# Slot product and inverse over n1 in the layer's two PSUM banks, with the products of the transform gathered behind the logits

## The chip, the cores and the metric

The kernel runs on one core of one Trainium2 chip. The metric is the device time of one execution in microseconds (us); lower is better. TensorE (PE) multiplies, ScalarE (ACT), VectorE (DVE) and GpSimd (POOL) work elementwise, SyncE (SP) issues the transfers. Each engine has its own list of instructions, and semaphores tie them together.

## The reference

The input is a batch of 8 sequences of 3072 tokens with 256 features. A Fourier filter runs over each sequence, then a layer with squared ReLU, then a mixture of experts with soft slots, whose softmax over all 24576 tokens decides what goes into each of 32 slots:

```python
X = np.fft.rfft(x, axis=1)
y = np.fft.irfft(X * F, n=x.shape[1], axis=1)          # filter, per sequence
h = np.maximum(x @ w_in, 0.0)                          # x: 24576 x 256
x = (h * h @ w_out)                                    # 24576 x 256
logits = x @ phi                                       # 24576 x 32
d = softmax(logits, axis=0); slot_input = d.T @ x      # slots from all tokens
...                                                    # 8 experts on 4 slots each
c = softmax(logits, axis=1); out = c @ slot_out
```

## The kernel before, in words

A sequence of 3072 = 128 x 24 tokens is transformed in two steps: over n1 (128 points) and over n2 (24 points), each a matrix product on TensorE. The way there is `mm_a` (over n1) and `mm_b` (over n2), then the filter is applied (`filt` on DVE, `join` on POOL), and the way back is `mm_g2` (over n2) and `mm_y` (over n1). Between `mm_a` and `mm_b` and between `mm_g2` and `mm_y` the data goes out to HBM and comes back in another order (`store_a`, `load_s2`, `store_g2`, `load_g`). Sequence 0 has a path of its own at the start; sequences 1 to 7 are transformed while the layer works on the sequence before.

The layer takes chunks of 512 tokens, 48 in all, and in each chunk 8 pairs P of 128-wide blocks of the hidden features. For each of the two blocks k of a pair, six full-array products (lines L594 to L596; `layer`) sum into PSUM bank `p0` or `p1`, of which there is one each. `square` then reads the bank: ReLU on ACT (L601), and the square on ACT for k = 0 (L603), on POOL for k = 1 (L605). The next pair's product for the same k waits until L601 has read the bank. DVE transposes the squares (`turn_h`, L622), and `logit` (L663) multiplies them with a folded weight; it uses 32 columns of the array at a time, four products side by side. `mm_b`, `mm_g2`, `mm_a`, `mm_y` and `slot_in` also divide the array, each in its own shape.

Per chunk c there is further work (`dispatch_events`): `evac_l`, `gather`, `emax`, `expo`, `turn_l`, `turn_e` make the weights of the softmax, `slot_in` (L794) multiplies them with the squares, which SP has moved into another layout (`move`), and `accum` (L855, DVE) adds the result to a running sum. `mm_y` (L514) gives the next chunk's input: `even_y` (L522, ACT) copies one half, `unfold` (L531, DVE) makes sum and difference, `lead_y` (L539, ACT) and `rest_y` (L546, POOL) split the result into a high and a low part.

The order is written by hand in a time of its own: a pair lasts 2 units, a chunk 16, a sequence 96. `put(t, fn, ...)` places a step at time t. `pair` calls `run_streams` before and after each of its four parts; it issues what is due, and a step with a product only where enough of the five spare PSUM banks (`side`) are free, by the table `take`. The logits of a chunk stand at times 1.5 and 9.5 (modulo 16); at 9.5 `slot_in` and `mm_y` follow them. The three products `mm_a` of a sequence, its four pairs of `mm_b` and its four `mm_g2` are placed by the numbers in `when`, and the loads that belong to them stand `LEAD` units earlier.

Of the kernel before, what the change touches and what calls it, by code (L numbers as in the profile page):

```python
# [6 lines left out]
F32 = mybir.dt.float32  # L7
# [13 lines left out]
CH = 512  # L21
NCB = N // CH
NCH = NB * NCB
# [15 lines left out]
def body(tc, x, cA, cAf, fwp, fwd, ivp, inv, flt, cst, w_in, w_out, phi, w1, w2, out):  # L39
# [10 lines left out]
    G = {}  # L50
# [32 lines left out]
    def put0(t, fn, *a):  # L83
        ev0[round(t, 3)].append((fn, a))
# [24 lines left out]
    def side():  # L109
        if G["nsd"]:  # L110
            return G["ps"].tile([128, 512], F32, tag="sd", name="sd", bufs=G["nsd"])
        k = free.pop(0)
        p = G["ps"].tile([128, 512], F32, tag=f"s{k}", name="sd")
        taken[id(p)] = k, p
        return p
# [7 lines left out]
    def fft_events(b, pl, put, TA, TB, TG, n, st):  # L123
# [263 lines left out]
        if b == 0:  # L387
# [21 lines left out]
            for i in range(8):  # L409
                put((.38, .4, .42, .44)[i] if i < 4 else F(i - 4) + 2.6, load_f, i)  # L410
                T = (16.8, 17.2, 20, 22.4, 24.9, 25.3, 27.4, 27.8)[i]
# [9 lines left out]
                T = (31.1, 33.6, 36.1, 38.6, 41.2, 44.7, 45.9, 42.4)[i]  # L421
# [5 lines left out]
        for s, (TL, TF, T) in enumerate(TA):  # L427
            put(TL, load_x, s)
            for k in range(2):
                put(TF + k, fold_x, s, k)  # L430
                for g in range(2):
                    put(T + 0.5 + (0 if T % 16 == 6 else 0.5) * k, evac_a, s, k, g)
                put(T + 2 + 0.5 * k, store_a, s, k)
            put(T, mm_a, s)
        LW, LV, LF, LS = n["lead"]
        for j in range(4):
            T = TB[j]
            for k in range(2):
                i = 2 * j + k
                put(T - LW[j], load_w, i)  # L440
                put(T, mm_b, i)
                for r in range(2):
                    put(T + 0.5 + 2 * k + r, filt, i, r)
                    put(T + 1 + 2 * k + r, join, i, r)
                put(TG[j] - LV[j], load_v, i)
            put(T - LF[j], load_f2, j)
            put(T - LS[j], load_s2, j)
            T = TG[j]
            put(T, mm_g2, j)
            for c in range(4):  # L450
                put(T + 0.5 + 0.5 * (c // 2), evac_g2, j, c)
            put(T + 3, store_g2, j)

    def out_events(b, st, late):

# [47 lines left out]

        def mm_y(g):
            t = st["gi", g]
            st["y", g] = p = [side() for e in range(2)]
            for a in range(4):
                for k in range(2):
                    for e in range(2):
                        for d in range(2):  # L510
                            rows = slice(64 * e, 64 * e + 64)
                            o = 128 * k + 64 * d
                            y = p[e][64 * d:64 * d + 64, D * k:D * k + D]
                            pe.matmul(  # L514
                                y.rearrange("p (q a t) -> p a q t", q=2, a=4)[:, a], t[rows, a, o:o + 64],
                                cI[rows, 0:64],
                                start=True, stop=True, skip_group_check=True, tile_position=(64 * e, 64 * d),
                            )
# [29 lines left out]
        for g in range(NCB):  # L548
            if 6 * b + g not in (0, 1, 6):
                T = 96 * b + 16 * g - 6.5  # L550
                late(max(T - 19.5, 13.5), load_g, g)
                late(T, mm_y, g)
                late(T + 0.5, even_y, g)
                late(T + 1, unfold, g, ALU.add)
                late(T + 1, unfold, g, ALU.subtract)
                for k in range(2):
                    late(T + 2 + 2 * k, lead_y, g, k)
                    late(T + 2.5 + 2 * k, rest_y, g, k)
                continue
            T = 96 * b + 16 * g - 4  # L560
            put = late
            if T < 0:
                def put(t, fn, *a):
                    put0(ST["G0"] + ST["Gd"] * (t + 7), fn, *a)
            put(T - (3 if T < 0 else 5), load_g, g)
            if T < 0:
                put(T - 1, warm)
            for k in range(2):
                put(T + k, mm_ai, g, k)
                put(T + k + 0.5, lead_ai, g, k)  # L570
                put(T + k + 0.5, rest_ai, g, k)
# [126 lines left out]
    def dispatch_events(c, put):  # L698
        q = 16 * (c + 1) + (2 if c else 6)
        st = {}  # L700
# [84 lines left out]

        def slot_in():

            st["S"] = S = side()
            e, h = st["eT"], hd.pop(c)
            for t in range(4):  # L790
                for n in range(4):
                    o = 4 * (n % 2)
                    v = h[:, n // 2, :, o:o + 4, 32 * t:32 * t + 32].rearrange("p r f j -> p f r j")
                    pe.matmul(  # L794
                        S[32 * n:32 * n + 32, :], e[:, 32 * t:32 * t + 32], v,
                        start=(t == 0), stop=(t == 3), tile_position=(0, 32 * n),
                    )
# [90 lines left out]
        if c == 0:  # L888
            for t, fn in zip(FIRST, (evac_l, gather, emax, expo, turn_l, turn_e, slot_blocks)):
                put(t, fn)  # L890
        else:
            put(q + .5, evac_l)
            put(q + 1.5, gather)
            put(q + 2.5, emax)
            put(q + 4, expo)
            put(q + 4, turn_l)
            put(q + 5, rescale)
            put(q + 5.5, turn_e)
        if c == 0:
            for r in range(4):  # L900
                put(FIRST[-1] + 1 + .5 * r, keep_block, r)
            put(FIRST[-1] + 3.5, sum_blocks)
        else:
            put(q + 7.5, slot_in)
            put(q + 9, accum)
        put(q + 11, row_max)
        put(q + 13, row_exp)
        put(q + 14, row_out)
# [118 lines left out]
    streams = {"dsp": [], "mv": [], "late": [], "fft": [], "w": []}  # L1027
    heads = dict.fromkeys(streams, 0)

    take = {"warm": 1, "mm_a": 4, "mm_b": 2, "mm_g": 4, "mm_g2": 4, "mm_ai": 1, "mm_y": 2, "gather": 1, "slot_in": 1, "slot_blocks": 4, "sum_blocks": 1, "turn_wo": 1, "mm_wf": 1}  # L1030

    def takes(fn, a):
        if fn is conv_wo and a[1] in (6, 7, 10):
# [3 lines left out]
    def stream(nm, o=0):  # L1037
        def put(t, fn, *a):
            streams[nm].append((t + o, fn, a))
        return put  # L1040
# [68 lines left out]
    with tc.manual_schedule():  # L1109
        put, late = stream("fft"), stream("late")  # L1110
        st = {}
        put0(43.3, load_const)
        fft_events(0, lambda: first, put0, 0, 0, 0, None, st)
        out_events(0, st, late)
        def wput(t, *a):

# [18 lines left out]
        for n in range(4):  # L1135
# [2 lines left out]
                wput(WO[n][1][k], conv_wo, n, k)  # L1138

        LEAD = [  # L1140
            [[6.5, 6.5, 9.5, 9.5], [10, 7.5, 8, 10], [5, 6, 6.5, 6.5], [5.5, 10.5, 10, 10]],
            [[5.5, 7.5, 15.25, 15.25], [6.5, 12.5, 13.5, 13.5], [5, 5.5, 10, 10], [5.5, 13, 15.25, 15.25]],
            [[20.25] + [15.25] * 3, [13.5] * 4, [20.5, 10, 10, 10], [8, 15.25, 15.25, 15.25]],
        ]

        opened = False
# [6 lines left out]
        for b in range(1, NB):  # L1153
            st = {}
            if b == 1:
                when = ([(22, 24.5, 26.5), (24, 29, 33.5), (27.5, 32, 36.5)], [47, 54.5, 65.5, 76.5], [53, 61.5, 70.5, 81.5])
            elif b == 2:
                when = ([(-19, -15.5, -10), (-11, -7, -3), (-5.5, -3, 0)], [13.5, 22, 38, 54], [18.5, 33.5, 49.5, 65.5])
            else:
                when = ([(-41, -31, -26), (-28, -22.5, -14.5), (-22.5, -15.5, -10)], [1.5, 22, 38, 54], [17.5, 33.5, 49.5, 65.5])  # L1160
            fft_events(b, lambda: G["fft"], stream("fft", 96 * (b - 1)), *when, dict(f=3, u=8, c=2, lead=LEAD[min(b, 3) - 1]), st)
            out_events(b, st, late)
        for c in range(NCH - 1):
            dispatch_events(c, stream("dsp"))
            if c:
                for n in range(4):
                    t = 0.5 * (n // 2)
                    for q, p in enumerate((12.5, 13.5, 14.5, 18) if c == 1 else (10, 11, 14, 18)):
                        stream("mv", 16 * c)(p + t, move, c, q, n)
# [10 lines left out]
        def bank(tag):  # L1180
            return G["ps"].tile([128, 512], F32, tag=tag, name="pt")
# [41 lines left out]
        for P in range(NP + 2):  # L1223
# [16 lines left out]
            if P > NP - 8:  # L1240
                j, odd = divmod(P - NP + 7, 2)
# [18 lines left out]
            evac_l, gather, emax, expo, rescale, turn_e, turn_l, slot_blocks, keep_block, sum_block,  # L1260
            row_max, row_exp, row_out, store_c,
        ) = dispatch_events(NCH - 1, None)
        zt = mlp.tile([128, NE, 8, NS], F32, tag="xo", name="zt", bufs=2)
        evac_l()
# [37 lines left out]
        for r in range(4):  # L1302
            p = st["S"][r]
# [13 lines left out]
        p = bank("p0")  # L1317
# [8 lines left out]
        p = bank("s1")  # L1326
# [65 lines left out]
        p = bank("s4")  # L1392
# [12 lines left out]
        for g in range(NG):  # L1405
            b, o = divmod(g, N2 // 4)
# [3 lines left out]
            for h in range(2):  # L1410
                p = bank(("s0", "s1", "s2", "s3")[ops % 4]).rearrange("p (a d) -> p a d", d=D)
# [166 lines left out]
```

## Time and profile before

| | |
|---|---|
| median of 3 runs | 1836.87 us (1836.69 to 1838.3) |
| the profiled execution | 1835.65 us, its span 1833.9 us |
| PE busy | 1804.7 us, 98% of the span |
| DVE, ACT, POOL busy | 65%, 56%, 43% |
| mean granted TensorE clock | 0.999 |

The span runs from the first to the last instruction of the trace; 1.75 us of the execution lie outside it. Busy time of PE is modelled (a product's end is worked out, and products overlap), so what a product costs is read from start to start.

### The profile page before, as it was taken

How to read it: one execution, taken by the hardware profiler on the slowest of the kernel's cores; microseconds unless marked ns; L12 is line 12 of the kernel's file. 1: busy time of each engine (PE TensorE's matmuls, PEld its weight loads, DVE VectorE, ACT ScalarE, POOL GpSimd, SP SyncE). 2: the span in 40 equal slices, each digit the busy share in tenths (PEclk: the TensorE clock that was granted, in tenths of full speed). 3: DMA queues.
4: the chain of work that ended last, by engine and by line, in shares of the span. 5: the costliest groups of instructions: out<-in, count | busy, mean ns of one | idle time of the engine just before them, and what ended most of it. 6: DMA issues, size and time to landing. Idle time of an engine off the chain costs nothing.

```text
span 1833.9 us, 42128 instructions
## 1 busy us (share of the span) xinstructions
PE 1804.7 (98%) x16326; PEld 1192.0 (65%) x16326; DVE 1199.4 (65%) x2264; ACT 1035.1 (56%) x1930; POOL 781.2 (43%) x815
## 2 busy tenths in 40 slices
PE   9999999999999999999999999999999999999986
PEld 7666666666666666666666666666666676666555
DVE  7956666676666666666667666666576756565568
ACT  6755555555555564555655565556555565555545
POOL 4144553444444534544444444444354533333234
PEclk9999999999999999999999999999999999999999
DMA  9779889888877896887978798788878666675989
GB/s 314 214 186 279 259 234 259 258 223 227 248 213 200 227 275 182 232 238 211 260 210 222 204 259 230 194 234 222 259 201 234 193 179 176 171 205 151 304 307 378
DMA packets 239846, 425.03 MB, mean 232 GB/s; under 512 B 25888, under 2 KB 95136, under 8 KB 239648
## 3 DMA queue, kind: packets, MB, share of 16 engines
q1 hardware_dynamic: 238776, 421.13, 79.3%
q8 instruction: 130, 2.13, 0.5%
q10 hardware_dynamic: 728, 1.15, 0.2%
q14 instruction: 68, 0.56, 0.1%
q0 software_dynamic: 144, 0.07, 0.0%
HBM read 151.71 MB, written 77.59 MB: 125 GB/s over the span
## 4 chain that ended last, share of the span: by engine, by line
PE 95%; DVE 2%; issue 1%; DMA 1%; ACT 1%; POOL 0%; SPq 0%; ACTq 0%; DVEq 0%; POOLq 0%
PE p L594 21%; PE p L596 19%; PE p L595 19%; PE L L663 10%; PE sd L794 9%; PE sd L299 3%; PE sd L218 3%; PE sd L514 3%; PE sd L165 2%; DVE ct L1212 1%; PE pt L1201 1%; PE sd L265 1%; PE pt L1414 1%; PE sd L339 1%; PE sd L724 1%
## 5 line engine op out<-in xcount | busy, mean ns | idle before, releaser
L605 POOL TENSOR_TENSOR h<-h 128x512 f32<-128x512 f32 x375 | 392.5, 1047 | 735.4 <-ACT h L601 681.5
L601 ACT ACTIVATE h<-p 128x512 f32<-128x512 f32 x768 | 459.0, 598 | 332.6 <-PE p L596 319.6
L622 DVE STREAM_TRANSPOSE hT<-h 128x512 f32<-128x512 f32 x736 | 485.2, 691 | 243.9 <-ACT h L603 230.9
L594 PE MATMUL p<-xo,wiH 128*128 128x512 f32 x1534 | 621.9, 405 | 0.2
L596 PE MATMUL p<-xo,wiL 128*128 128x512 f32 x1534 | 605.9, 395 | 0.6 <-DVE wiL L980 0.6
L595 PE MATMUL p<-xo,wiH 128*128 128x512 f32 x1534 | 605.1, 394 | 0.0
L594 PEld LDWEIGHTS p<-xo,wiH 128*128 128x128 f32 x1534 | 288.1, 188 | 123.6 <-issue 44.3
L596 PEld LDWEIGHTS p<-xo,wiL 128*128 128x128 f32 x1534 | 288.3, 188 | 69.8 <-DVE wiL L980 1.1
L595 PEld LDWEIGHTS p<-xo,wiH 128*128 128x128 f32 x1534 | 288.6, 188 | 60.7
L603 ACT ACTIVATE h<-h 128x512 f32<-128x512 f32 x393 | 248.4, 632 | 12.5
L319 POOL TENSOR_TENSOR u<-u 128x256 f32<-128x256 f32 x224 | 160.4, 738 | 110.9 <-DVE u L310 110.9
L663 PE MATMUL L<-h,wf 128*32 128x512 f32 x1536 | 186.9, 599 | 0.4 <-ACT h L603 0.4
L531 DVE TENSOR_TENSOR gin<-gin,sd 128x512 f32<-128x512 f32 x90 | 61.8, 687 | 179.5 <-ACT gin L522 177.9
L522 ACT ACTIVATE gin<-sd 128x512 f32<-128x512 f32 x45 | 26.9, 598 | 256.4 <-PE sd L514 256.4
L794 PE MATMUL sd<-hd,eT 128*32 128x512 f32 x1472 | 166.4, 592 | 0.0
L310 DVE TENSOR_TENSOR u<-sd,f 128x512 f32<-128x512 f32 x240 | 152.7, 674 | 10.4 <-PE sd L299 9.0
L794 PEld LDWEIGHTS sd<-hd,eT 128*32 128x32 f32 x1472 | 48.0, 110 | 109.9 <-issue 106.1
L546 POOL TENSOR_TENSOR xo<-gin,xo 128x512 fp32r<-128x512 f32 x90 | 119.2, 1324 | 0.0
L713 DVE TENSOR_TENSOR lo<-L,lp 128x512 fp32r<-128x512 f32 x47 | 32.3, 687 | 114.5 <-ACT lp L712 114.5
L228 ACT ACTIVATE f<-sd 128x512 f32<-128x512 f32 x112 | 61.1, 610 | 80.0 <-PE sd L218 80.0
L663 PEld LDWEIGHTS L<-h,wf 128*32 128x32 f32 x1536 | 40.0, 109 | 93.9 <-issue 92.1
L156 POOL TENSOR_TENSOR f<-f 128x512 f32<-128x512 f32 x42 | 54.3, 1294 | 67.4 <-DVE u L155 48.1
(162 smaller groups left out, 1599.5 us busy)
## 6 DMA issues: line engine op xcount, KB each, us to landing
hd<-hT SPq DMA_DIRECT2D x736, 256.0 KB
f<-flt SPq DMA_DIRECT2D x28, 1024.0 KB
gin<-G SPq DMA_DIRECT2D x47, 512.0 KB
out<-w1t SPq DMA_DIRECT2D x47, 512.0 KB
f<-x SPq DMA_DIRECT2D x84, 256.0 KB
S<-f SPq DMA_DIRECT2D x42, 512.0 KB
f<-S SPq DMA_DIRECT2D x112, 192.0 KB
G<-f SPq DMA_DIRECT2D x112, 192.0 KB
```

Of the source, the lines that this page charges most:

```text
L310: vec.tensor_tensor(out=u, in0=p.rearrange("p (h d) -> p h d", d=D), in1=f[:, 2 * r + k:2 * r + k + 1, :].to_broadcast([128, 2, D]), op=AL ...
L319: gps.tensor_tensor(out=a[:, h, :], in0=a[:, h, :], in1=b[:, 1 - h, :], op=ALU.add if h else ALU.subtract)
L546: gps.tensor_tensor(out=lo, in0=st["gi", g][:, k::2, :], in1=hi, op=ALU.subtract)
L594: pe.matmul(p, wh, x[:, 0, kk, :], start=(kk == 0), stop=False)
L595: pe.matmul(p, wh, x[:, 1, kk, :], start=False, stop=False)
L596: pe.matmul(p, wl, x[:, 0, kk, :], start=False, stop=(kk == 1))
L601: act.activation(out=h, in_=p, func=ACTF.Relu, scale=2.0 ** -8)
L603: act.activation(out=h, in_=h, func=ACTF.Square)
L605: gps.tensor_tensor(out=h, in0=h, in1=h, op=ALU.mult)
L622: vec.transpose(hT[c, f // 8][:, f // 4 % 2, :, o:o + 128], h2[P, k].rearrange("p (b t) -> p b t", b=4))
L663: pe.matmul(lg[c][32 * n:32 * n + 32, :], wf[:, f, :], h2.pop((P + n // 2, n % 2)), start=(f < 4), stop=(f >= FT - 4), tile_position=(0, 3 ...
L794: pe.matmul(S[32 * n:32 * n + 32, :], e[:, 32 * t:32 * t + 32], v, start=(t == 0), stop=(t == 3), tile_position=(0, 32 * n),)
```

## The change: what it does

`slot_in` writes into bank `p0` and one half of `mm_y` into `p1`, the banks of the layer, in place of spare banks. `accum` is placed at 7.6 in place of 9 of the chunk's own time, right behind `slot_in`. With the spare banks that this leaves, `mm_g2` moves to 9.5 (modulo 16), behind `slot_in` and `mm_y`, and `mm_b` moves to 1.5, behind the logits; the middle `mm_a` of a sequence moves to 9.5 and the two others to 1.5. What empties the banks of these products is spread over more units (`mid`). `lead_y` and `rest_y` move forward: both `lead_y` to the unit of `unfold`. `turn_l` moves back by 2.5 units, and the lead times of the loads change.

```diff
             for k in range(2):
                 put(TF + k, fold_x, s, k)
+                mid = T % 16 == 9.5
                 for g in range(2):
-                    put(T + 0.5 + (0 if T % 16 == 6 else 0.5) * k, evac_a, s, k, g)
-                put(T + 2 + 0.5 * k, store_a, s, k)
+                    put(T + (2 + 2 * k if mid else 0.5 + (0 if T % 16 == 6 else 0.5) * k), evac_a, s, k, g)
+                put(T + (2.5 + 2 * k if mid else 2 + 0.5 * k), store_a, s, k)
...
-                    put(T + 0.5 + 2 * k + r, filt, i, r)
-                    put(T + 1 + 2 * k + r, join, i, r)
+                    t = T + ((0.5, 2, 4, 6.5)[2 * k + r] if T % 16 == 1.5 else 0.5 + (2 * k + r) * (0.5 if 6 <= T % 16 < 7 else 1))
+                    put(t, filt, i, r)
+                    put(t + 0.5, join, i, r)
...
+            mid = T % 16 == 9.5 and b > 1
             for c in range(4):
-                put(T + 0.5 + 0.5 * (c // 2), evac_g2, j, c)
-            put(T + 3, store_g2, j)
+                put(T + ((2, 4, 5, 6)[c] if mid else 0.5 + 0.5 * (c // 2)), evac_g2, j, c)
+            put(T + (6.5 if mid else 3), store_g2, j)
...
-            st["y", g] = p = [side() for e in range(2)]
+            st["y", g] = p = [G["ps"].tile([128, CH], F32, tag="p1", name="y"), side()]
...
                 for k in range(2):
-                    late(T + 2 + 2 * k, lead_y, g, k)
-                    late(T + 2.5 + 2 * k, rest_y, g, k)
+                    late(T + 1, lead_y, g, k)
+                    late(T + 1.5 + 0.5 * k, rest_y, g, k)
...
-            st["S"] = S = side()
+            st["S"] = S = G["ps"].tile([128, CH], F32, tag="p0", name="S")
...
-            put(q + 4, turn_l)
+            put(q + (6.5 if c < NCH - 2 else 4), turn_l)
...
             put(q + 7.5, slot_in)
-            put(q + 9, accum)
+            put(q + 7.6, accum)
...
-"mm_y": 2, "gather": 1, "slot_in": 1,
+"mm_y": 1, "gather": 1, "slot_in": 0.5,
...
         LEAD = [
-            [[6.5, 6.5, 9.5, 9.5], [10, 7.5, 8, 10], [5, 6, 6.5, 6.5], [5.5, 10.5, 10, 10]],
-            [[5.5, 7.5, 15.25, 15.25], [6.5, 12.5, 13.5, 13.5], [5, 5.5, 10, 10], [5.5, 13, 15.25, 15.25]],
-            [[20.25] + [15.25] * 3, [13.5] * 4, [20.5, 10, 10, 10], [8, 15.25, 15.25, 15.25]],
+            [[6.5, 6.5, 9.5, 9.5], [10, 3.5, 8, 7.5], [5, 6, 6.5, 6.5], [5.5, 10.5, 10, 10]],
+            [[5.5, 7.5, 10.5, 12.5], [6.5, 6, 6, 6], [5, 5.5, 7.25, 8.25], [5.5, 13, 10.5, 13.5]],
+            [[12.5] * 4, [6] * 4, [12, 8.25, 8.25, 8.25], [8.5, 13.5, 13.5, 13.5]],
         ]
...
-                when = (..., [47, 54.5, 65.5, 76.5], [53, 61.5, 70.5, 81.5])
+                when = (..., [47, 54.5, 65.5, 76.5], [53, 57.5, 73.5, 81.5])
...
-                when = ([(-19, -15.5, -10), (-11, -7, -3), (-5.5, -3, 0)], [13.5, 22, 38, 54], [18.5, 33.5, 49.5, 65.5])
+                when = ([(-19, -15.5, -10), (-11, -7, -3), (-5.5, -3, 1.5)], [13.5, 22, 33.5, 49.5], [18.5, 25.5, 41.5, 57.5])
...
-                when = ([(-41, -31, -26), (-28, -22.5, -14.5), (-22.5, -15.5, -10)], [1.5, 22, 38, 54], [17.5, 33.5, 49.5, 65.5])
+                when = ([(-45, -38.75, -30.5), (-38.75, -29, -22.5), (-25.5, -22, -14.5)], [1.5, 17.5, 33.5, 49.5], [9.5, 25.5, 41.5, 57.5])
```

PE's list, before, at one of the `mm_b` (L299) in the middle of the program; L594 to L596 are the layer, and `L299 ... x32` is the whole product.

```order
L594 MATMUL p<-xo,wiH 128x512
L595 MATMUL p<-xo,wiH 128x512
L596 MATMUL p<-xo,wiL 128x512
L299 MATMUL sd<-f_9546,fw 32x256 x32
L594 MATMUL p<-xo,wiH 128x512
L595 MATMUL p<-xo,wiH 128x512
```

In the changed kernel an `mm_b` reads so in PE's list (line numbers are 3 higher from the layer on; L666 is `logit`):

```order
L597 MATMUL p<-xo,wiH 128x512
L598 MATMUL p<-xo,wiH 128x512
L599 MATMUL p<-xo,wiL 128x512
L666 MATMUL L<-h,wf 32x512 x8
L299 MATMUL sd<-f_13559,fw 32x256 x32
L597 MATMUL p<-xo,wiH 128x512
```

The product no longer parts two layer products; it follows the logits. Over the program the places where a layer product is followed directly by `mm_b`, `mm_a` or `mm_g2` go from 22, 14 and 4 to 5, 3 and 2. Of the 45 `mm_y`, all were followed by the layer; now 25 are followed by `mm_g2`, 5 by `mm_a`, and 15 still by the layer: 8 in the earlier sequences (one in six chunks from the third sequence on), and 7 in the last, which has no transform beside it. At the first of the 15 an `mm_a` stands between the first and the second bank of the next pair. `slot_in` is followed by the layer, without `mm_y`, twice in both.

ACT's list, before, around the last `even_y` (L522), whose `mm_y` the layer follows; L601 and L603 are the ReLU and the square, L539 is `lead_y`, and `xo` is the next chunk's input.

```order
L601 ACTIVATE h<-p 128x512
L522 ACTIVATE gin<-sd 128x512
L601 ACTIVATE h<-p 128x512
L603 ACTIVATE h<-h 128x512
L539 ACTIVATE xo<-gin 128x512
L601 ACTIVATE h<-p 128x512 x2
L603 ACTIVATE h<-h 128x512
L539 ACTIVATE xo<-gin 128x512
L601 ACTIVATE h<-p 128x512 x2
```

The same place in the changed kernel (L604, L606, L525, L542 are the same four):

```order
L604 ACTIVATE h<-p 128x512
L525 ACTIVATE gin<-y 128x512
L542 ACTIVATE xo<-gin 128x512 x2
L604 ACTIVATE h<-p 128x512
L606 ACTIVATE h<-h 128x512
L604 ACTIVATE h<-p 128x512 x2
L606 ACTIVATE h<-h 128x512
```

Both `lead_y` moved ahead of the first ReLU of the pair that follows. This order is the same behind every `mm_y`.

DVE's list, before, around one of the `accum` (L855, L856) of the last sequence; L531 is `unfold`, L622 `turn_h`, L780 `row_max`.

```order
L622 STREAM_TRANSPOSE hT<-h 128x4x128 x3
L531 TENSOR_TENSOR gin<-gin,sd 128x512 x2
L855 SCALAR_TENSOR_TENSOR ac<-ac,sc,sd 128x512
L856 SCALAR_TENSOR_TENSOR z<-z,sc,zb 128x1
L622 STREAM_TRANSPOSE hT<-h 128x4x128 x2
L780 TENSOR_REDUCE rm<-lt 128x4
```

And in the changed kernel (L763 is `turn_l`, L534 `unfold`, L858 and L859 `accum`, which now reads bank `S`):

```order
L625 STREAM_TRANSPOSE hT<-h 128x4x128
L763 STREAM_TRANSPOSE lt<-sd 32x128 x4
L625 STREAM_TRANSPOSE hT<-h 128x4x128 x2
L858 SCALAR_TENSOR_TENSOR ac<-ac,sc,S 128x512
L859 SCALAR_TENSOR_TENSOR z<-z,sc,zb 128x1
L534 TENSOR_TENSOR gin<-gin,sd 128x512 x2
L625 STREAM_TRANSPOSE hT<-h 128x4x128 x2
```

`accum` moved ahead of `unfold`, and `turn_l` stands directly ahead of it.

## Rows read from the trace of the kernel before

**Rows 1.** The page: busy time by engine, then the chain that ended last, by engine.

```profile
PE 1804.7 (98%) x16326; PEld 1192.0 (65%) x16326; DVE 1199.4 (65%) x2264; ACT 1035.1 (56%) x1930; POOL 781.2 (43%) x815
...
PE 95%; DVE 2%; issue 1%; DMA 1%; ACT 1%; POOL 0%; SPq 0%; ACTq 0%; DVEq 0%; POOLq 0%
```

**Rows 2.** Windows: length, busy us of PE, PEld, DVE, ACT, POOL, clock, DMA share.

```profile
300.00:510.50 210.50, 210.50 (x1972) 137.28 (x1971) 139.22 (x261) 117.32 (x217) 99.00 (x104) 1.00 0.87 239
```

**Rows 3.** Timeline of PE (start, length, us) around an mm_b between layer products.

```profile
576.79 0.40 PE L595 MATMUL p<-xo,wiH 128*128 128x512 f32 x1
577.02 0.40 PE L596 MATMUL p<-xo,wiL 128*128 128x512 f32 x1
577.35 1.96 PE L299 MATMUL sd<-f,fw 48*32 48x256 f32 x64
579.24 0.50 PE L594 MATMUL p<-xo,wiH 128*128 128x512 f32 x1
579.58 0.39 PE L595 MATMUL p<-xo,wiH 128*128 128x512 f32 x1
```

**Rows 4.** Timeline of PE: two logit groups of one chunk, and what follows.

```profile
708.38 1.93 PE L663 MATMUL L<-h,wf 128*32 128x512 f32 x16
710.24 1.96 PE L299 MATMUL sd<-f,fw 48*32 48x256 f32 x64
...
723.94 1.92 PE L663 MATMUL L<-h,wf 128*32 128x512 f32 x16
725.68 3.62 PE L794 MATMUL sd<-hd,eT 128*32 128x512 f32 x32
729.23 1.16 PE L514 MATMUL sd<-cst_t,gin 64*64 64x64 f32 x64
730.32 0.50 PE L594 MATMUL p<-xo,wiH 128*128 128x512 f32 x1
...
733.22 0.40 PE L594 MATMUL p<-xo,wiH 128*128 128x512 f32 x1
```

**Rows 5.** Timeline of ACT, then of DVE, behind the mm_y of rows 4.

```profile
730.49 0.60 ACT L522 ACTIVATE gin<-sd 128x512 f32<-128x512 f32 x1 [5.78 <-PE sd L514]
732.02 0.60 ACT L601 ACTIVATE h<-p 128x512 f32<-128x512 f32 x1 [0.93 <-PE p L596]
733.19 0.61 ACT L539 ACTIVATE xo<-gin 128x512 fp32r<-128x512 f32 x1
733.71 0.58 ACT L601 ACTIVATE h<-p 128x512 f32<-128x512 f32 x1
...
731.12 1.41 DVE L531 TENSOR_TENSOR gin<-gin,sd 128x512 f32<-128x512 f32 x2 [4.89 <-ACT gin L522]
```

**Rows 6.** Timeline of ACT, then of PE (PEld: its weight loads), at a wait for a ReLU.

```profile
124.43 0.62 ACT L539 ACTIVATE xo<-gin 128x512 fp32r<-128x512 f32 x1
124.95 0.59 ACT L601 ACTIVATE h<-p 128x512 f32<-128x512 f32 x1
...
125.59 0.19 PEld L594 LDWEIGHTS p<-xo,wiH 128*128 128x128 f32 x1 [0.48 <-ACT h L601]
125.59 0.50 PE L594 MATMUL p<-xo,wiH 128*128 128x512 f32 x1
```

**Rows 7.** Timeline: layer and accum behind one of the two slot_in without mm_y.

```profile
268.76 0.50 PE L594 MATMUL p<-xo,wiH 128*128 128x512 f32 x1
268.90 0.75 DVE L855 SCALAR_TENSOR_TENSOR ac<-ac,sc,sd 128x512 f32<-128x512 f32 x1 [0.76 <-PE sd L794]
```

**Rows 8.** Timeline of PE: a usual mm_g2, then a late mm_a.

```profile
323.95 1.98 PE L218 MATMUL sd<-u,iv 32*64 32x256 f32 x64
325.86 0.50 PE L594 MATMUL p<-xo,wiH 128*128 128x512 f32 x1
...
281.89 0.65 PE L165 MATMUL sd<-u,ca_t 64*64 64x512 f32 x2
284.71 0.50 PE L594 MATMUL p<-xo,wiH 128*128 128x512 f32 x1
```

More of the change, by code (lines that the diff above doesn't have):

```diff
@@ L1028, in body @@
     heads = dict.fromkeys(streams, 0)
-    take = {"warm": 1, "mm_a": 4, "mm_b": 2, "mm_g": 4, "mm_g2": 4, "mm_ai": 1, "mm_y": 2, "gather": 1, "slot_in": 1, "slot_blocks": 4, "sum_blocks": 1, "turn_wo": 1, "mm_wf": 1}
+    take = {"warm": 1, "mm_a": 4, "mm_b": 2, "mm_g": 4, "mm_g2": 4, "mm_ai": 1, "mm_y": 1, "gather": 1, "slot_in": 0.5, "slot_blocks": 4, "sum_blocks": 1, "turn_wo": 1, "mm_wf": 1}
     def takes(fn, a):
@@ L1155, in body @@
             if b == 1:
-                when = ([(22, 24.5, 26.5), (24, 29, 33.5), (27.5, 32, 36.5)], [47, 54.5, 65.5, 76.5], [53, 61.5, 70.5, 81.5])
+                when = ([(22, 24.5, 26.5), (24, 29, 33.5), (27.5, 32, 36.5)], [47, 54.5, 65.5, 76.5], [53, 57.5, 73.5, 81.5])
             elif b == 2:
-                when = ([(-19, -15.5, -10), (-11, -7, -3), (-5.5, -3, 0)], [13.5, 22, 38, 54], [18.5, 33.5, 49.5, 65.5])
+                when = ([(-19, -15.5, -10), (-11, -7, -3), (-5.5, -3, 1.5)], [13.5, 22, 33.5, 49.5], [18.5, 25.5, 41.5, 57.5])
             else:
-                when = ([(-41, -31, -26), (-28, -22.5, -14.5), (-22.5, -15.5, -10)], [1.5, 22, 38, 54], [17.5, 33.5, 49.5, 65.5])
+                when = ([(-45, -38.75, -30.5), (-38.75, -29, -22.5), (-25.5, -22, -14.5)], [1.5, 17.5, 33.5, 49.5], [9.5, 25.5, 41.5, 57.5])
             fft_events(b, lambda: G["fft"], stream("fft", 96 * (b - 1)), *when, dict(f=3, u=8, c=2, lead=LEAD[min(b, 3) - 1]), st)
```

## The prediction, made before the run

> **What bounds the kernel now.** I read the page first. PE is busy for 1804.7 us of a span of 1833.9, DVE for 65%, ACT for 56%, and the chain of work that ended last is PE for 95% [rows 1]. A window over one whole sequence (210.5 us, 96 units of the program's time) has PE busy in every part of it, at a granted clock of 1.00, with ACT at 117.3 us and DVE at 139.2 us [rows 2]. So in the steady part the list of PE is the bound, and there are two ways for a new order to change the time: products follow each other more or less closely, or PE comes to wait for something for which it does not wait now. Busy time shows neither, since a product's end is modelled. I therefore read starts.
>
> Next comes the timeline of PE at the products that the change moves. In the layer a product starts 0.23 us after the one before (576.79 to 577.02). The last one ahead of `mm_b` takes 0.33 us to the next start, and the first one behind it takes 0.34 us (579.24 to 579.58) [rows 3]. So a product that parts the layer costs, beyond its own 1.89 us, 0.10 us on the way in and 0.11 us on the way back. Behind a group that is there anyway, it costs neither.
>
> Last come the lists of ACT and DVE behind `mm_y`, since the change reorders them, and PE has one bank for each k of the layer.
>
> **The joined products.** From the order: 40 products stand alone between layer products (22 + 14 + 4), and 10 will (5 + 3 + 2). 30 times 0.20 us is 6.0 us less. What the joined products cost inside the group is not shown for all pairs. `mm_b`, `mm_a` and `mm_g2` have stood behind logits before, and the logits take 1.86 us to the next start there (708.38 to 710.24) [rows 4], which stays. `mm_g2` behind `mm_y` (25 times) and `mm_a` behind `mm_y` (5 times) are new. Now the layer starts 1.09 us after `mm_y` (729.23 to 730.32) [rows 4], and I take the same for both, since the shape changes in either case. Bounds: logits take 1.74 us where `slot_in`, of the same shape, follows, and 1.86 us where another shape does [rows 4]; so 0.12 us either way, 30 times, is 3.6 us to both sides.
>
> [...]
>
> **The layer behind `mm_y`.** This is the dearest part. Where the layer follows `mm_y`, ACT's list now reads `even_y`, ReLU of (P5,0) (P5 is the pair that follows, 0 its bank `p0`), square, `lead_y`. Then it will read `even_y`, both `lead_y`, ReLU. An engine goes through its list in order: at 124.43 us a `lead_y` ran ahead of a ReLU on ACT, the ReLU ended at 125.54, and the layer went on at 125.59, with ACT's L601 named as what ended the idle time [rows 6]. That is the same wait in small, and it gives 0.05 us from ACT's end to PE's start.
>
> What the ReLU will wait for, in one such place: `even_y` runs from 730.49 to 731.09. `unfold` needs it, and its two parts end at 732.53. `lead_y` reads both parts, so it can start at about 732.58. On ACT the next instruction starts 0.52 us after a copy (733.19 to 733.71) [rows 5], so two copies put the ReLU at 733.62 and its end, 0.60 us on, at 734.22. Now it starts at 732.02 [rows 5]. The second product into `p0` starts at 733.22 now [rows 4] and needs that ReLU; it will start at 734.27, 1.05 us later. A wait lets the array run empty, so I add 0.10 us for the slower first product, as in rows 3: 1.15 us in all. Bank `p1` then causes no second wait: the square and the ReLU of (P5,1) follow at 0.52 us each, so that ReLU ends at about 735.3, and its bank is needed six products of 0.23 us and the 0.10 us after 734.27, at about 735.7.
>
> This price is paid only where nothing stands between `mm_y` and the layer. With an `mm_g2` of 1.91 us (323.95 to 325.86) [rows 8] the products of (P5,0) end 1.91 us later, the ReLU can start at 733.93 at the earliest, and ACT is free at 733.62: no wait, with 0.3 us to spare. For `mm_a` in that place I take the same length. By the order 15 `mm_y` are followed by the layer; in the first of them an `mm_a` comes between the banks and covers the wait. So 14 times 1.15 us, 16.1 us more.
>
> **`slot_in` in `p0`.** The layer cannot start in `p0` until `accum` has read it. Behind an `mm_y` that is covered: DVE's list has `accum` ahead of `unfold`, it would start about 0.14 us after `mm_y` does, the lag that rows 7 show behind a `slot_in`, take 0.75 us, and the layer starts after 1.09 us. The cover is thin (0.15 us with the 0.05 us of rows 6), and it goes if DVE is late. In the two places without `mm_y` nothing covers it: the layer starts at 268.76 and `accum` runs from 268.90 to 269.65 [rows 7]; with 0.05 us on top the layer starts at 269.70, 0.94 us later. I take the other place to be alike. Together 1.9 us more. The half of `mm_y` in `p1` is read by `even_y` alone, which ends at 731.09, and `p1` is wanted six layer products after 730.32, some 1.5 us on: nothing.
>
> **Late inputs.** An `mm_a` of the third sequence takes 2.82 us (281.89 to 284.71) [rows 8], against 1.9 us for the other products of the transform [rows 3, 8]; I read this as a late input. It moves back by 1.5 units behind logits, and I take off 0.9 us. If that is wrong it is nothing.
>
> **Moved steps that I cost at nothing.** The copies out of `mm_g2` now stand one to a ReLU pair; per pair ACT then has two ReLUs, a square and a copy, four starts of 0.52 us, or 2.1 us, against 12 layer products of 0.23 us, 2.8 us. If two copies fell between two ReLUs the margin would be gone. `filt` moves nearer to the logits, so DVE does four of them, `turn_e` and `turn_l` ahead of `slot_in`, in a stretch that the logits and `slot_in` lengthen by 5.3 us (723.94 to 729.23) [rows 4]. On SP the loads are issued later and stand ahead of the moves; the moves must wait for `slot_in` anyway, so what is ahead of them has that time to land.
>
> **The sum**, against the profiled execution's 1835.65 us: less 6.0, plus 16.1, plus 1.9, less 0.9, gives 1846.75 us. That execution lies 1.2 us below the median of the runs (1836.87), so I forecast **1848 us**, slower by 0.6%. A change of 0.2% (3.7 us) is about what runs of this kernel can tell from none.
>
> **The rivals.**
>
> 1. *The wait does not arise, the joins pay.* This would be so if the ReLU of (P5,0) were free of the two `lead_y`, by timing: it decides at 733.17, the end of that ReLU that the next product into `p0` can bear. `unfold` would have to end 1.05 us sooner. For it speaks that ACT is idle 44% of the time; against it, that DVE already does the two parts back to back, straight behind `even_y` [rows 5]. Then 1835.65 - 6.0 + 1.9 - 0.9 is 1830.7, or 1832 against the median: faster.
> 2. *The groups with `mm_g2` wait too.* The spare 0.3 us on ACT and 0.15 us on DVE are thin. If DVE reaches `accum` or `unfold` about 1 us late there, 25 groups pay some 0.8 us each: 20 us more, 1868. DVE has 34% free in the window [rows 2], which speaks against.
> 3. *Transfers come late.* Lead times shrink while the transfer engines are busy at a share of 0.87 [rows 2]. A late input costs about 0.9 us as in rows 8; if half of the 23 joined `mm_b` pay it, that is 10 us more, 1858.
> 4. *Nothing to see.* The wait is real but smaller: at 0.5 us for each of the 14 the sum is 7.0 + 1.9 - 6.0 - 0.9, 2 us, 1839.
>
> **How the numbers follow.** My forecast has a chance of 0.62, its own range 1843 to 1854 (the 3.6 us of the joins and 0.1 us on each wait, either way). Rival 1 has 0.14, rival 2 0.08, rival 3 0.07, rival 4 0.09. Faster by over 0.2% is rival 1: 0.14. Within 0.2% is most of rival 4: 0.08. The rest, 0.78, is slower. The range goes from 1831.5, which takes in most of rival 1, to 1856, which leaves out rival 2 and the larger part of rival 3.
>
> **What would show it.** In the changed profile: PE waits on ACT's ReLU about 1.05 us long, 14 of them, half in the last sequence, each six plus six layer products behind an `mm_y`; two waits on `accum` of about 0.9 us; no wait behind a group with `mm_g2`; an `mm_b` that starts straight behind the logits, with the logits still 1.86 us long. The span of the last sequence alone should be some 9 us longer (7 waits and one `accum`), and a middle sequence some 0.2 us longer or even (5 joins less at 0.2 us each, one wait more). Wrong would be: ReLUs of ACT that do not end late behind those `mm_y`, or waits in the 25 groups that I take as covered.

## The result, and the profile after

The changed kernel takes 1854.78 us (median of 5 runs, 1852.55 to 1857.3) against 1836.87 us before: a ratio of 1.0093, 95% interval [1.0082, 1.0104]. It is slower by 0.9%. The profiled executions are 1852.71 and 1835.65 us, 17.1 us apart, where the sum of the prediction had 11.1 us.

The page of the changed kernel, busy time by engine and then the chain that ended last, answers to [rows 1]:

```profile
PE 1805.0 (98%) x16326; PEld 1192.4 (64%) x16326; DVE 1205.6 (65%) x2264; ACT 1042.7 (56%) x1930; POOL 778.5 (42%) x815
...
PE 89%; DVE 4%; ACT 3%; DMA 2%; issue 1%; POOL 0%; SPq 0%; DVEq 0%; ACTq 0%; POOLq 0%
```

PE is busy for the same time as before (1804.7 us) in a span that is 17.0 us longer, so PE waits. More of the chain runs through ACT and DVE. The list of waits of PE says for what (engine and line, what was waited for, us in all, times, the longest):

```profile
PE p L597 <- ACT h L604: 13.2, 16, 0.8
PE pt L1204 <- DVE ct L1215: 6.1, 21, 0.6
PE p L597 <- DVE ac L858: 1.7, 2, 0.9
```

Sixteen waits of the layer (L597) for a ReLU (L604) and two for `accum` (L858); the row between them is of the last stage, as before. One of the sixteen, in the last sequence: ACT's timeline, then PE's.

```profile
1510.76 0.60 ACT L525 ACTIVATE gin<-y 128x512 f32<-128x512 f32 x1 [5.75 <-PE sd L517]
1512.83 1.15 ACT L542 ACTIVATE xo<-gin 128x512 fp32r<-128x512 f32 x2 [1.47 <-DVE gin L534]
1513.89 0.58 ACT L604 ACTIVATE h<-p 128x512 f32<-128x512 f32 x1
...
1510.62 0.50 PE L597 MATMUL p<-xo,wiH 128*128 128x512 f32 x1
...
1514.52 0.50 PE L597 MATMUL p<-xo,wiH 128*128 128x512 f32 x1 [0.84 <-ACT h L604]
```

It reads as the prediction drew it from [rows 5, 6]: `even_y`, then ACT idle until `unfold` is done, both `lead_y`, and only then the ReLU, which ends at 1514.47. PE takes up the next six products into `p0` at 1514.52. The last of the six products into `p0` ahead of that had started at 1511.89, and ACT stood idle for 1.47 us with the ReLU behind it in its list.

**A ledger.** The layer has 4608 products in both traces, so the start of the n-th in the one can be set against the n-th in the other. The difference grows to 17.60 us at the last of them (0.6 us of it is made up in the final stage), and each of its steps has a place:

| step | predicted, us | measured, us |
|---|---|---|
| the joins, 30 (measured without the one three rows below) | -6.0 | -6.7 |
| 14 waits for the ReLU, 1.00 + 0.11 us each | +16.1 | +15.5 |
| 2 waits for `accum`, 0.94 and 0.93 us | +1.9 | +1.9 |
| the late `mm_a` of the third sequence, with its join | -0.9 | -0.35 |
| two groups of sequence 1's transform, 0.99 us each | 0 | +2.0 |
| the first of the 15 places, in `slot_blocks` | 0 | +0.7 |
| five groups with `mm_a`, 0.19 + 0.10 us each | 0 | +1.4 |
| three `mm_g2` that stop in the middle | 0 | +2.5 |
| start-up: first layer product +0.5, two `gather` +1.2, waits in `mm_b` and `logit` gone -1.1 | 0 | +0.6 |

### The profile page after: what moved, and what is told of

It reads as the page before. It is cut to its first block, busy times and chain, and to the rows that moved or that the text cites. A ratio compares the mean times of both kernels' runs of the same rounds, so it can differ in the third digit from the quotient of the medians.

```text
span 1850.9 us, 41894 instructions
## 1 busy us (share of the span) xinstructions
PE 1805.0 (98%) x16326; PEld 1192.4 (64%) x16326; DVE 1205.6 (65%) x2264; ACT 1042.7 (56%) x1930; POOL 778.5 (42%) x815
## 4 chain that ended last, share of the span: by engine, by line
PE 89%; DVE 4%; ACT 3%; DMA 2%; issue 1%; POOL 0%; SPq 0%; DVEq 0%; ACTq 0%; POOLq 0%
PE p L597 19%; PE p L599 18%; PE p L598 18%; PE L L666 10%; PE S L797 9%; PE sd L218 3%; PE sd L299 3%; PE y L517 2%; PE sd L165 2%; DVE gin L534 1%; ACT xo L542 1%; DMA f<-flt 1%; DVE ct L1215 1%; PE pt L1204 1%; DMA wt<-w_in 1%
## 5 line engine op out<-in xcount | busy, mean ns | idle before, releaser
L625 DVE STREAM_TRANSPOSE hT<-h 128x512 f32<-128x512 f32 x736 | 490.6, 694 | 360.4 <-ACT h L606 343.1
L604 ACT ACTIVATE h<-p 128x512 f32<-128x512 f32 x768 | 458.8, 597 | 320.6 <-PE p L599 302.5
L597 PE MATMUL p<-xo,wiH 128*128 128x512 f32 x1534 | 621.2, 405 | 15.1 <-ACT h L604 13.2
L597 PEld LDWEIGHTS p<-xo,wiH 128*128 128x128 f32 x1534 | 288.2, 188 | 146.2 <-issue 33.8
L606 ACT ACTIVATE h<-h 128x512 f32<-128x512 f32 x393 | 248.4, 632 | 12.5
L319 POOL TENSOR_TENSOR u<-u 128x256 f32<-128x256 f32 x224 | 160.4, 738 | 133.4 <-DVE u L310 117.2
L549 POOL TENSOR_TENSOR xo<-gin,xo 128x512 fp32r<-128x512 f32 x90 | 114.4, 1290 | 216.8 <-ACT xo L542 216.8
L666 PE MATMUL L<-h,wf 128*32 128x512 f32 x1536 | 187.1, 599 | 0.4 <-ACT h L606 0.4
L525 ACT ACTIVATE gin<-y 128x512 f32<-128x512 f32 x45 | 26.9, 598 | 255.1 <-PE sd L517 255.1
L797 PE MATMUL S<-hd,eT 128*32 128x512 f32 x1472 | 166.3, 592 | 0.0
L797 PEld LDWEIGHTS S<-hd,eT 128*32 128x32 f32 x1472 | 47.8, 110 | 110.1 <-issue 110.1
L666 PEld LDWEIGHTS L<-h,wf 128*32 128x32 f32 x1536 | 40.0, 109 | 94.1 <-issue 92.1
L858 DVE SCALAR_TENSOR_TENSOR ac<-ac,sc,S 128x512 f32<-128x512 f32 x46 | 34.4, 747 | 88.5 <-PE S L797 88.5
L542 ACT ACTIVATE xo<-gin 128x512 fp32r<-128x512 f32 x90 | 51.9, 624 | 64.2 <-DVE gin L534 64.2
L534 DVE TENSOR_TENSOR gin<-gin,sd 128x512 f32<-128x512 f32 x90 | 61.8, 687 | 35.7 <-ACT gin L525 34.1
```

Of the source, the lines that this page charges most:

```text
L319: gps.tensor_tensor(out=a[:, h, :], in0=a[:, h, :], in1=b[:, 1 - h, :], op=ALU.add if h else ALU.subtract)
L549: gps.tensor_tensor(out=lo, in0=st["gi", g][:, k::2, :], in1=hi, op=ALU.subtract)
L597: pe.matmul(p, wh, x[:, 0, kk, :], start=(kk == 0), stop=False)
L604: act.activation(out=h, in_=p, func=ACTF.Relu, scale=2.0 ** -8)
L606: act.activation(out=h, in_=h, func=ACTF.Square)
L625: vec.transpose(hT[c, f // 8][:, f // 4 % 2, :, o:o + 128], h2[P, k].rearrange("p (b t) -> p b t", b=4))
```

## The experiments

Each run is compared with runs of the kernel before on the same chip.

**1. Where the waits come from.** Both `lead_y` and `rest_y` back at their old times, in the changed kernel:

```diff
-                    late(T + 1, lead_y, g, k)
-                    late(T + 1.5 + 0.5 * k, rest_y, g, k)
+                    late(T + 2 + 2 * k, lead_y, g, k)
+                    late(T + 2.5 + 2 * k, rest_y, g, k)
```

> The changed kernel with both lead_y and both rest_y back at the times of before (2 and 4, 2.5 and 4.5 units behind mm_y); everything else stays changed. Theory A (the 14 waits of the layer come from the two lead_y that stand ahead of the ReLU on ACT): the 14 waits of 1.00 us with their 0.11 us of slower first product go, 15.5 us; the waits of 0.9 and 0.1 us in the two groups of the first transform where the copies out of mm_g2 stand there too go, 2.0 us; the five of 0.19 us behind mm_a go, 1.0 us. 1852.7 - 18.5 is 1834 us, 0.990 of the changed kernel, and no faster than before by more than 2 us. Rival B (the waits come from accum, which now stands ahead of unfold on DVE, or from mm_y in p1): the 14 waits stay, and the time is 1850 us or more.

Measured: 1849.4 us, ratio to before 1.0065 [1.0053, 1.0077]. All 14 waits are gone (0.00 us in each place), and so are the two in the groups of the first transform, so theory A holds for them. But the time did not fall to 1834 us. Where a product is joined there are new waits, 0.32 us in each of 23 groups with `mm_g2`, and 1.1 to 1.2 us in each of the five with `mm_a`: some 13 us. The five waits of 0.19 us, which I had expected to go, grew to 0.71 us. And in the profiled execution the `mm_g2` that stop (experiment 7) cost 2.7 us more than in that of the changed kernel. ACT's timeline in a group with `mm_g2`, then PE's:

```profile
528.06 0.60 ACT L604 ACTIVATE h<-p 128x512 f32<-128x512 f32 x1 [2.88 <-PE p L599]
528.69 0.63 ACT L606 ACTIVATE h<-h 128x512 f32<-128x512 f32 x1
529.23 0.62 ACT L542 ACTIVATE xo<-gin 128x512 fp32r<-128x512 f32 x1
529.75 0.58 ACT L228 ACTIVATE f<-sd 128x512 f32<-128x512 f32 x1
530.22 1.22 ACT L604 ACTIVATE h<-p 128x512 f32<-128x512 f32 x2
...
530.86 0.50 PE L597 MATMUL p<-xo,wiH 128*128 128x512 f32 x1
```

Now a `lead_y` (L542) and a copy out of `mm_g2` (L228) stand together between two ReLUs. The second ReLU, which frees `p1`, ends at 530.8. PE wants `p1` again 18 products of 0.233 us and 0.10 us after the layer's start at 526.36, at about 530.65, and starts at 530.86. The layer pays 0.2 us and 0.1 us for a slower first product; behind `mm_a` the wait is 0.7 us. The prediction had named this for the copies ("if two copies fell between two ReLUs the margin would be gone"), but not that it is the reason why `lead_y` cannot simply stay late.

**2. Late only where nothing is joined.**

```diff
-                    late(T + 1, lead_y, g, k)
-                    late(T + 1.5 + 0.5 * k, rest_y, g, k)
+                    joined = 1 + (b == 1) <= g <= 4 and 1 <= b <= 6 or g == 5 and 1 <= b <= 5
+                    late(T + (1 if joined else 2 + 2 * k), lead_y, g, k)
+                    late(T + (1.5 + 0.5 * k if joined else 2.5 + 2 * k), rest_y, g, k)
```

> The changed kernel with lead_y and rest_y at the times of before only where the layer follows mm_y directly and in the two groups of the first transform; behind the groups that hold an mm_g2 or mm_a of a later sequence they stay early. Theory A: 15.5 and 2.0 us less than the changed kernel, 1835 us, and PE waits for a ReLU in none of those places; the five waits of 0.19 us stay. If the copies out of mm_g2 and lead_y hinder each other on ACT when both are late, this kernel is faster than the one with all lead_y late; by theory A alone it is 1 us slower. Rival B: 1850 us or more.

Measured: 1836.07 us, 0.9992 [0.9983, 1.0001] of before: within 1 us of theory A's 1835 us, with no wait of the layer for a ReLU but the five of 0.19 us. Most of the step from experiment 1 to this one, 13.3 us, is what the two kinds of copies cost each other on ACT.

**3. The early `lead_y` alone**, in the kernel before (the two lines of experiment 1 the other way round, and nothing else).

> The kernel before with nothing changed but the times of lead_y and rest_y, which are those of the change (1, 1.5 and 2 units behind mm_y). There the layer follows all 45 mm_y directly. Theory A: 44 or 45 waits of 1.00 us and 0.11 us for the slower first product, 48 to 50 us more: about 1884 us (1875 to 1888). Rival B (the order of accum and unfold, or the banks, make the waits): no change, 1836 us.

Measured: 1887.31 us in one run. PE's waits:

```profile
PE p L594 <- ACT h L601: 37.8, 44, 0.9
```

There are 44 steps of some 1.0 us, 49.5 us with the slower first products. One edit of two lines makes the wait wherever the layer follows `mm_y`, without banks and joins.

**4. The banks alone**, in the kernel before.

```diff
-            st["y", g] = p = [side() for e in range(2)]
+            st["y", g] = p = [G["ps"].tile([128, CH], F32, tag="p1", name="y"), side()]
-            st["S"] = S = side()
+            st["S"] = S = G["ps"].tile([128, CH], F32, tag="p0", name="S")
-            put(q + 9, accum)
+            put(q + 7.6, accum)
```

> The kernel before with the two banks alone: slot_in into p0, one half of mm_y into p1, accum at 7.6. No product is moved and lead_y stays where it was. The sum of the prediction gives 1.9 us more (0.94 us in each of the two places where slot_in is followed by the layer): 1837.5 us for the profiled run, a ratio of 1.001 to before. The rival that the banks cost in each of the 45 groups (the 0.15 us of cover on accum gone): some 0.2 us in each, 9 us more, 1846 us.

Measured: 1837.84 us, 1.0004 [0.9995, 1.0012], and in PE's waits the two for `accum` alone:

```profile
PE p L594 <- DVE ac L855: 1.7, 2, 0.9
```

No group pays for the bank behind an `mm_y`: the difference in the start of the layer's products stays at 3.41 us from the eighth `slot_in` to the last, over 38 groups. So the 0.15 us of cover, thin as they are, hold. The 1.9 us are too small to show in the time, but the trace shows them.

**5. One `lead_y` ahead of the ReLU, not two** (changed kernel, `lead_y` at T + 1 + 2k, `rest_y` at T + 1.5 + 2k).

> The changed kernel, but with the second lead_y and rest_y two units later than the first, so that one copy, not two, stands ahead of the ReLU. Theory A: each of the 14 waits falls by one copy of 0.52 us, from 1.00 to about 0.48 us, 7.3 us less; but where mm_g2 or mm_a is joined the second lead_y then stands with a copy out of the product between two ReLUs, which cost up to 0.35 us in each of some 20 groups in the run with both late. 1845 to 1852 us. Rival B: the 14 waits stay at 1.00 us.

Measured: 1848.25 us in one run. Each of the 14 steps is 0.48 or 0.49 us, down from 1.00 us by one copy of 0.52 us; 8.2 us in all with the slower first products. In the two groups of the first transform the step falls from 0.9 to 0.37 us. Size follows cause one to one. The other half of the expectation failed: the groups with `mm_g2` pay nothing for the second `lead_y`, and only the five with `mm_a` pay, 0.34 us each.

**6. `slot_in` in a spare bank where no `mm_y` follows**, on top of experiment 2.

```diff
-            st["S"] = S = G["ps"].tile([128, CH], F32, tag="p0", name="S")
+            st["S"] = S = side() if c in (4, NCH - 2) else G["ps"].tile([128, CH], F32, tag="p0", name="S")
```

> The kernel with lead_y late in the bare places, and besides slot_in in a spare bank in the two places where no mm_y follows it. Theory: the two waits of the layer for accum, 0.94 us each, go, and nothing else changes: 1.9 us less than that kernel's 1836.1 us, 1834.2 us, 0.9985 of before. If slot_in in a spare bank delays the products behind it there, the gain is smaller.

Measured: 1835.18 us, 0.9988 [0.9978, 0.9998]. The two steps of 0.94 and 0.96 us are 0.01 us or less now. This version beats the changed kernel clearly and the kernel before by 0.12%, with an interval that ends just short of no difference.

**7. The `mm_g2` that stop.** In the changed kernel three of the joined `mm_g2` halt amid their 64 products, between two that read the same tiles. PE's timeline at one:

```profile
1054.51 1.08 PE L218 MATMUL sd<-u,iv 32*64 32x256 f32 x20
1056.12 1.54 PE L218 MATMUL sd<-u,iv 32*64 32x256 f32 x44 [0.53 <-issue]
```

And the DMA queue of the instructions in the stretch from 1053.2 to 1054.6 (packets, MB, share of 16 engines):

```profile
q8 instruction: 1, 0.02, 5.8%
```

"issue" is a wait for nothing that the profile shows. The halts stand at the same products of PE in several executions: before the 4104th, 7984th and 9860th (counted from 0) in the changed kernel and in experiments 1, 2 and 5, at the 12988th in experiment 2, and at the 7232nd in experiment 5. Their length differs: in all 2.5 us in the changed kernel, 5.2 us in experiments 1 and 2, 6.7 us in experiment 5. The queue q8 moves 130 packets of 16384 bytes, and PE's list has some 33,400 instructions (16326 products, as many loads of weights, and the waits), 130.5 times 256. Counted so, all these products have the same rest on division by 256, 193. In the changed kernel PE goes on 2.6 to 2.9 us after the packet starts. So I took the code itself to be late, and shifted it, in the kernel of experiment 6: the six products that bridge a wait in the start-up became 38, or 22, narrower ones, which are 128 or 64 more instructions (each counts as two products and two loads in PE's list).

```diff
-            for _ in range(6):
-                pe.matmul(p[:, 0:416], cI, cst_t[:, 0:416], start=True, stop=True)
+            for _ in range(22):
+                pe.matmul(p[:, 0:112], cI, cst_t[:, 0:112], start=True, stop=True)
```

> The same kernel as e5, but the six products that keep PE busy while it waits for its first input are cut into 38 narrower ones (64 columns for 416), so that every later instruction of PE stands 128 instructions further back. Theory C: the stalls inside three or four mm_g2 (0.3 to 2.3 us each, at PE's products 4104, 7984, 9860 and 12988 of the profile in several kernels) are code that is loaded late, 256 instructions at a time; the block borders then fall 64 products earlier, into mm_y, and the stalls at those four products go. New ones may come in the 12 mm_g2 into which a border falls now; every stall then stands at a border that is shifted by 128 instructions, and PE goes on 2.4 to 2.9 us after the start of an instruction packet. Rival D (late inputs of these mm_g2, from filt or join): the stalls stay at the same products of the same mm_g2. Time by theory C: 1831 to 1836 us, by rival D as e5, 1834 us.

> As e6, with 22 products of 112 columns, which puts PE's later instructions 64 further back. Theory C: no stall at the four products, and those that come stand 32 products earlier in PE's list than a border of e5. Rival D: as e5.

Measured: with 64 instructions 1833.04 us, 0.9978 [0.9968, 0.9988]; with 128, 1843.05 us, 1.0025 [1.0012, 1.0038]. PE's timeline at the same `mm_g2` in experiment 6 and with 64 more instructions:

```profile
833.37 1.96 PE L218 MATMUL sd<-u,iv 32*64 32x256 f32 x59
836.10 0.65 PE L218 MATMUL sd<-u,iv 32*64 32x256 f32 x5 [0.77 <-issue]
```

```profile
836.82 1.10 PE L218 MATMUL sd<-u,iv 32*64 32x256 f32 x27
839.38 1.51 PE L218 MATMUL sd<-u,iv 32*64 32x256 f32 x37 [1.47 <-issue]
```

The halt moved from behind the 59th product to behind the 27th: 32 products and their 32 loads, the 64 instructions that were put in. In PE's list it is the 7983rd product both times. With 128 more, this `mm_g2` runs through in 1.98 us, and the two long halts (1.2 and 1.0 us) stand in other `mm_g2`, at a rest of 194. Theory C holds, rival D falls. That 128 more cost time has another cause. The 38 narrow products took 14.2 us in place of 4.5 us, and the granted clock, 1.00 until then, was 0.5 from 50.6 to 64.3 us, while the narrow ones ran from 48.0 us on. PE's timeline, then the window (its clock is the third number from the end):

```profile
48.04 14.20 PE L474 MATMUL sd<-cst_t 128*128 128x64 f32 x76 [1.31 <-ACT x L352]
...
50.60:64.30 13.70, 13.70 (x66) 13.70 (x66) 4.32 (x5) 1.40 (x3) 0.00 (x0) 0.50 0.33 112
```

The first layer product starts 9.9 us later than in experiment 6. Of the 12 executions with 128 more, seven have a mean granted clock of 0.994 or 0.995 and take 1842.8 to 1846.8 us; the other five, at 0.998 or 0.999, take 1836.2 to 1839.2 us. So most of the loss goes with the clock, and some 3 us against experiment 6 remain without it. Whether 64 more are better than none is open, as the intervals overlap.

**8. A version with `mm_g2` ahead of `slot_in`**, so that no two dense products stand together; its copies ahead of `even_y`, `lead_y` late everywhere. The core of the edit (`mid` of `evac_g2` and `evac_a` becomes 0.5):

```diff
-        for nm in streams:
+        for nm in sorted(streams, key=lambda nm: nm != "fft") if t % 16 in (9.5, 10) and t > 50 else streams:
```

> A version that should beat both. As e5 (slot_in in a spare bank where no mm_y follows), but at 9.5 the joined mm_g2 or mm_a stands ahead of slot_in, not behind mm_y, its copies stand on ACT ahead of even_y, and lead_y is late everywhere, as before the change. Theory C: 256 instructions of PE now always last 6 us or more (an mm_g2 of 1.9 us, a slot_in of 3.55 us and half an mm_y), so no block of code comes late and no mm_g2 stalls; no ReLU is late either, since no two copies stand between two of them and none ahead of the first. Against e5's median 1835.2: less 1.7 us (the stalls of its profiled run) to 5 us, less 1.0 us (five waits of 0.19 us behind mm_a): 1829 to 1833 us. Rival: an mm_g2 that starts 4.6 us sooner waits for join, up to 1 us in 25 places, or the logits ahead of slot_in cost 0.12 us each for the change of shape: 1836 us or more.

> As e9, with the four filt behind a joined mm_b at 0.5, 2, 3.5 and 5 units in place of 0.5, 2, 4 and 6.5, so that join ends earlier. If mm_g2 waits for join in e9, this one is faster than e9 by that wait; if not, it is the same within 1 us.

Measured: 1843.81 us, 1.0033 [1.002, 1.0045], and 1847.05 us, 1.0049 [1.0036, 1.0061]: a miss. PE's timeline in one group:

```profile
518.50 1.92 PE L666 MATMUL L<-h,wf 128*32 128x512 f32 x16
520.36 1.98 PE L218 MATMUL sd<-u,iv 32*64 32x256 f32 x64
522.27 3.64 PE L797 MATMUL S<-hd,eT 128*32 128x512 f32 x32
526.93 0.50 PE L597 MATMUL p<-xo,wiH 128*128 128x512 f32 x1
```

The logits take 1.86 us to the next start, where they took 1.74 us ahead of `slot_in`, which has their shape. From the first logit to the layer it is 8.43 us against 8.29 us in experiment 6: 0.14 us in each of 25 groups, and 0.30 us in five with `mm_a`, which the wait saved there (0.19 and 0.10 us) gives back. Of the layer's waits for a ReLU one of 0.5 us is left. But the halts did not go, as I had expected: they stand in `mm_y` now (1.5 and 0.9 us in two of them), at a rest of 193 or 194, and PE goes on 2.5 to 2.7 us after the packet starts. That 256 instructions take 6 us did not help: in these two the packet starts when 166 and 183 of the 256 instructions ahead of the border have already run. Why it starts no sooner, no run shows.

Some 6 us of the loss lie in the first 350 us. About half of them are what the rival of the expectation had named: in two groups `mm_g2`, which now starts sooner, stops for `join` (L319, POOL) or `filt`, which costs 2.1 us in the first and 1.1 us in the second. PE's timeline in the first:

```profile
190.01 2.01 PE L218 MATMUL sd<-u,iv 32*64 32x256 f32 x40
192.71 1.34 PE L218 MATMUL sd<-u,iv 32*64 32x256 f32 x24 [0.69 <-POOL u L319]
```

In the other 23 groups the profile shows no such wait. The second kernel could not help, since the `mm_b` ahead of these two groups do not stand at 1.5; the waits are no shorter in it. In its profiled execution the layer starts 6.1 us later, behind a load that came 3.7 us late.

## Why the prediction was right, and where not

The forecast itself came out on the low side: 1854.78 us lies just above its own range of 1843 to 1854 us (whose upper end should have been 1853 by the terms named there), and within the wider range only because that also makes room for rivals.

**The joins** were read rightly: -6.7 us against -6.0 us, and 0.5 us of the difference is the next point. Of the two prices for the parts inside a group, the row now shows both. `mm_g2` follows `mm_y` after 1.09 us, and `mm_a` follows it sooner:

```profile
455.46 0.27 PE L517 MATMUL y<-cst_t,gin 64*64 64x64 f32 x2
...
456.44 0.59 PE L165 MATMUL sd<-u,ca_t 64*64 64x512 f32 x1
```

That is 0.98 us, 0.11 us less. I had taken 1.09 us for both, "since the shape changes in either case"; but in the trace `mm_a` has the shape of `mm_y` (64*64), and `mm_g2` has another (32*64). It is worth 0.5 us in five places, and experiment 8 shows a like price, 0.14 us in each of 25 groups, where another shape follows the logits in place of `slot_in`.

**The wait for the ReLU** was the right step with the right size: 1.00 us and 0.11 us for the slower first product, against 1.05 and 0.10 us, in 14 places, 7 of them in the last sequence. At the one shown above the first product took 0.34 us to the next start (1514.52 to 1514.86) behind 0.84 us in which PE was idle, the second 0.23 us. The array run empty, to which the prediction laid this, the trace shows as that idle time alone. Experiments 1, 3 and 5 take it away, make it alone, and halve it. The last sequence is 8.4 us longer (9 forecast), and a middle one 0.24 to 0.27 us where no `mm_g2` halts (0.2 forecast).

**`slot_in` in `p0`** cost 1.87 us against 1.9 us, and nothing behind `mm_y` (experiments 4 and 6).

**What was missing** are some 7 us of terms that I had set to nothing; joins and waits 1.3 us cheaper than forecast hid part of it:

- "This price is paid only where nothing stands between `mm_y` and the layer" failed in two of 25 groups. The diff spreads the copies only for b > 1; in the first transform they stand in ACT's list around `lead_y`, ahead of the ReLU. ACT, then PE, there:

```profile
196.94 0.60 ACT L525 ACTIVATE gin<-y 128x512 f32<-128x512 f32 x1 [5.75 <-PE sd L517]
198.87 1.09 ACT L228 ACTIVATE f<-sd 128x512 f32<-128x512 f32 x2 [1.33 <-PE sd L218]
199.84 1.15 ACT L542 ACTIVATE xo<-gin 128x512 fp32r<-128x512 f32 x2
200.88 1.08 ACT L228 ACTIVATE f<-sd 128x512 f32<-128x512 f32 x2
201.83 0.62 ACT L604 ACTIVATE h<-p 128x512 f32<-128x512 f32 x1
...
202.50 0.50 PE L597 MATMUL p<-xo,wiH 128*128 128x512 f32 x1 [0.73 <-ACT h L604]
```

- "The copies out of `mm_g2` now stand one to a ReLU pair" holds behind the first transform, but I had not counted the copies out of `mm_a` (L172): two of them stand between two ReLUs, and by the prediction's own words the margin is then gone. ACT, then PE, in one of the five groups:

```profile
459.98 0.60 ACT L604 ACTIVATE h<-p 128x512 f32<-128x512 f32 x1
460.61 0.63 ACT L606 ACTIVATE h<-h 128x512 f32<-128x512 f32 x1
461.14 1.07 ACT L172 ACTIVATE f<-sd 128x512 f32<-128x512 f32 x2
462.10 1.27 ACT L604 ACTIVATE h<-p 128x512 f32<-128x512 f32 x2
...
462.75 0.50 PE L597 MATMUL p<-xo,wiH 128*128 128x512 f32 x1
```

The ReLU that frees `p1` starts at 462.10, and PE goes on 0.19 us late. With one copy fewer (0.48 us from start to start here) it would have been in time. The shorter cover behind `mm_y` (above) does no harm: the ReLU of `p0`, at 459.98, is followed by no wait.

- In the first of the 15 places `mm_a` did hide the wait of the layer, but the ReLU was late all the same, with it the square and `turn_h`, and `slot_blocks` took 5.42 us where it takes 4.39 us with `lead_y` late (0.7 us in the end).
- "I read this as a late input" ([rows 8]): the `mm_a` waited for POOL's part of `fold_x`. Moved back it no longer waits, but POOL runs that step ahead of a square, and a logit of the chunk waits for the square. Before, then in the changed kernel:

```profile
283.70 0.20 PEld L165 LDWEIGHTS sd<-f,ca_t 64*64 64x64 f32 x4 [0.76 <-POOL f L156]
...
288.06 1.29 POOL L156 TENSOR_TENSOR f<-f 128x512 f32<-128x512 f32 x1 [0.63 <-DVE u L155]
289.31 2.04 POOL L608 TENSOR_TENSOR h<-h 128x512 f32<-128x512 f32 x2
...
290.40 0.14 PEld L666 LDWEIGHTS L<-h,wf 128*32 128x32 f32 x2 [0.66 <-POOL h L608]
```

So the 0.9 us went to the next in POOL's list.

- Rival 3 had late transfers at about 1 us; transfers did come late, but those of PE's code, 2.5 us in three places. Before, PE never reached a block's border in the steady part sooner than 6.8 us after its packet had started; in the changed kernel the shortest there is 2.5 us. The halts go with the joined groups: experiments 3 and 4, without them, have none (shortest 6.8 and 4.1 us).

The start-up terms are not settled. The banks alone (experiment 4) start the layer 1.05 us later than before and hold the `gather` at 140 us for 0.8 us. In the changed kernel and experiments 1, 2, 5 and 6, whose first instructions are the same, the layer starts between 55.0 and 56.2 us, so these terms differ between executions.

## What to carry to other kernels

A step that is moved forward in an engine's list is paid by what then stands behind it (here 1.00 us where both `lead_y` stood ahead of the ReLU, 0.48 us where one did): count, at each place, what the next instruction in that list releases, and do it for the places that are exceptions (first sequence, last sequence, no neighbour), which held 20 of the 25 us lost here (15.5, 1.9, 2.0 and 0.7). A copy has a right place only in relation to the other copies of its group: early where another product gives cover, late where it does not. And dense runs of small products can get ahead of their code: here that cost 2.5 to 6.7 us.

## What the runs showed of the hardware

PE's instructions came in packets of 16384 bytes, one for about 256 (130 packets, some 33,400 instructions), and in twelve profiled executions PE passed no border between two blocks sooner than 2.3 us after the start of the packet. Where it reached one sooner it halted, for up to 2.3 us (experiment 1). In the kernel before and in experiments 3 and 4, whose products are not joined, no halt shows.
